# Nineteen folded columns a head for twenty: the last softmax feature of keys and queries set to one by GpSimd

## The chip, the cores and the metric

One core of a Trainium2 chip runs the whole program. The time is device microseconds of one execution, inputs and outputs in HBM; the figure of a kernel is the median over its runs. The core's engines, with the names that the profile uses: TensorE (PE, with its weight loads PEld), VectorE (DVE), ScalarE (ACT), GpSimd (POOL) and SyncE (SP, which here issues nearly all DMAs).

## The reference

Two residual blocks over x of 2048 tokens by 640: linear attention with a softmax feature map (32 heads of 20), then a dense SiLU block of width 1728.

```python
qkv = x @ wqkv                                  # layernormed x; 32 heads, Dh = 20
pq = jnp.einsum("bhsd,hdf->bhsf", q, w_phi)     # 20 features a head
pk = jnp.einsum("bhsd,hdf->bhsf", k, w_phi)
phi_q = concat([softmax(pq), softmax(-pq)])     # 40 features a head
phi_k = concat([softmax(pk), softmax(-pk)])
kv = jnp.einsum("bhsf,bhsd->bhfd", phi_k, v)
z  = jnp.einsum("bhsf->bhf", phi_k)
o  = (phi_q @ kv) / (phi_q . z + 1e-6)
h  = x + o.reshape(B, S, D) @ wo
out = h + silu(layernorm(h) @ w1) @ w2
```

## The kernel before, in words

The tokens are 16 tiles of 128. For each tile t the first part does: moments and normalization of x (`st`, `rs`, `xn`), a transpose into XnT (`xt`; by PE for the first four tiles, by a DMA on SP for the others), keys' features by PE (`K`), two exponentials of them by ACT (`ex`, exp and exp of the negative), the sums over each 20 by DVE (`su`), their inverse by ACT (`rk`), the scaling by DVE (`sc`), the values by PE with a copy by ACT (`V`, `ve`), and the product of scaled features and values, accumulated over all tiles in PSUM (`kv`). Queries go the same way (`Q`, `qe`, `qs`, `ql`, `qi`, `qr`, `qt`), then attention (`D`, `E`), the output projection (`ot`, `G`, `ga`), the second layernorm (`ls`, `lr`, `hn`, `ht`) and the dense block (`u`, `s`, `d`, `oa`, `out`).

The features need no separate step for w_phi: it is folded into the key and query columns of wqkv ahead of time. For keys, PE transposes Wk (`wk`), DVE builds a block-diagonal `phi` from w_phi (`phi_a`, `phi_b`), and PE multiplies both into Wfk (`fk`, copied by `fk..e`). For queries the same is done in six blocks of up to 120 columns: POOL builds `phi_q` (`phq`), PE multiplies with the DMA-transposed WTq (`fq`, L400), ACT or DVE copies into Wfq (`fq..e`, L406).

What is emitted when is written out by hand in ORDER, a list of step names; each step's instructions go to the in-order queues of their engines at that place, and semaphores for what one needs of another are set from the tiles that they read and write. So an instruction that waits holds whatever stands behind it on its engine. Of the steps around the change: xn3 to xn5 and xn7 to xn15 are on POOL, L450.

Buffers that matter here: the exponentials of a key tile go to `EK[t % 4]` (NE = 4), laid out as 64 runs of 20 features (32 heads, plus and minus) and a zeroed tail; `su` (L557) and `sc` (L570) work on all 20 of a run, and `kv` (L589) reads the scaled buffer as its weights. `VP[t % 8]` holds the values, with a column of ones for each head that POOL writes once for a buffer (`ones0` to `ones7`, L229); `kv` multiplies by it, so that z comes out beside kv. The queries' exponentials go to EQ, which has a place for each of the 16 tiles. PSUM has eight banks; until the queries' halves are used, `K`, `V`, `Q`, `fk` and `fq` take pairs of banks in turn out of three pairs, so that each waits for whoever reads the pair's content of three takers before.

Of the kernel before, what the change touches and what calls it, by code (L numbers as in the profile page):

```python
# [59 lines left out]
def kernel(  # L60
# [20 lines left out]
    DH = 20  # L81
    HF = 2 * DH
# [142 lines left out]
    Wfk = proj.tile([P, C, D], BF16, name="Wfk")  # L225
    Wfq = proj.tile([P, C, D + DH], BF16, name="Wfq")

    def ones(i):
        nc.gpsimd.memset(VP[i][:, :, DH:HV], 1.0)  # L229
        if i < NE:  # L230
            nc.gpsimd.memset(EK[i][:, H * HF :], 0.0)

# [25 lines left out]
    BW = 240  # L258

    PB = {0: (0, 240, 0), 1: (120, 260, BW), 2: (240, 400, 2 * BW), 3: (380, 520, 3 * BW + 20), 4: (400, 640, 4 * BW - 80)}  # L260
# [12 lines left out]
    nc.gpsimd.memset(phi[:, :, 8 * DH : BW], 0.0)  # L273
    ps_of = {}

    def phi_own(b):

        a, n = 3 * b, 3 - b
        engines[on(f"phi_{'ab'[b]}", "DVE")].tensor_tensor(
            phi[:, a : a + n, 0 : 8 * DH].rearrange("p r (h f) -> p r h f", f=DH),  # L280
            WPH[:, a : a + n].unsqueeze(2).to_broadcast([P, n, 8, DH]),
            own[:, a : a + n].unsqueeze(3).to_broadcast([P, n, 8, DH]), op=ALU.mult,
        )
# [53 lines left out]
    LW = D - (NQ - 1) * QW  # L337
    WPQ = early.tile([P, NQ, DH], BF16, name="WPQ")
    own_q = early.tile([P, 2, BH], BF16, name="own_q")
    phi_q = early.tile([P, NQ, QW], BF16, name="phi_q")  # L340
# [25 lines left out]
    def phi_blocks():  # L366

        n = NQ - 1
        nc.gpsimd.tensor_tensor(
            phi_q[0:QW, 0:n].rearrange("p r (h f) -> p r h f", f=DH),  # L370
            WPQ[0:QW, 0:n].unsqueeze(2).to_broadcast([QW, n, BH, DH]),
            own_q[0:QW, 0].unsqueeze(1).unsqueeze(3).to_broadcast([QW, n, BH, DH]), op=ALU.mult,
        )
        n = LW // DH
        nc.gpsimd.tensor_tensor(
            phi_q[P // 2 : P, NQ - 1, 0:LW].rearrange("p (h f) -> p h f", f=DH),
            WPQ[P // 2 : P, NQ - 1].unsqueeze(1).to_broadcast([P // 2, n, DH]),
            own_q[P // 2 : P, 1, 0:n].unsqueeze(2).to_broadcast([P // 2, n, DH]), op=ALU.mult,
        )
# [10 lines left out]
    def width(r):  # L390
        return min(QW, D - QW * r)
# [13 lines left out]
    def folded_block(eng, r):  # L405
        eng(Wfq[:, :, QW * r : QW * r + width(r)], ps_of.pop(("fq", r)))  # L406
# [12 lines left out]

    add("eqp", eq_pads)  # L420

# [71 lines left out]
    def project(t, W, key):  # L493

        ps = ps_of[key, t] = ps_pair()
        for g in range(2):
            for c in range(C):
                nc.tensor.matmul(  # L498
                    ps[:, g, 0:HD],
                    XnT[:, c, t * P : (t + 1) * P],  # L500
                    W[:, c, g * HD : (g + 1) * HD],
                    start=(c == 0),
                    stop=(c == C - 1),
                )
# [27 lines left out]
    def project_queries(t, g, ps):  # L532
        a, b = (DH * h for h in Q_PARTS[g])
        for c in range(C):
            e = b if c == 0 else min(b, D)
            nc.tensor.matmul(  # L536
                ps[:, 0 : e - a], XnT[:, c, t * P : (t + 1) * P], Wfq[:, c, a:e],
                start=(c == 0), stop=(c == C - 1),
            )
# [8 lines left out]
    def key_exps(t):  # L548
        ek[t] = EK[t % NE]
        p4 = ps_of.pop(("K", t))[:, :, 0:HD].rearrange("p g (h f) -> p g h f", f=DH)  # L550
        E5 = ek[t][:, 0 : H * HF].rearrange("p (g h b f) -> p g h b f", g=2, b=2, f=DH)
        for b, sign in ((0, 1.0), (1, -1.0)):
            nc.scalar.activation(E5[:, :, :, b, :], p4, AF.Exp, scale=sign)  # L553
# [51 lines left out]
    for t in range(T):  # L605
        if t == 0:
            add("K0s", first_key_bank)
            for c in range(C):
                add(f"K0.{c}", lambda c=c: first_key_chunk(c))
        else:  # L610
            add(f"K{t}", lambda t=t: project(t, Wfk, "K"))
        add(f"ex{t}", lambda t=t: key_exps(t))
        add(f"su{t}", lambda t=t: key_sums(t))
        add(f"rk{t}", lambda t=t: key_inverse(t))
        add(f"sc{t}", lambda t=t: key_scale(t))
        if t == 0:
# [27 lines left out]
    def query_exps(t):  # L644

        n = DH * HC
# [8 lines left out]
        for a, b, ps in parts:  # L655
            p4 = ps.rearrange("p (c h f) -> p c h f", h=HC, f=DH)
            for i, sign in ((0, 1.0), (1, -1.0)):
                nc.scalar.activation(features(t, a, b)[:, :, :, i], p4, AF.Exp, scale=sign)  # L658
# [308 lines left out]
```

## Time and profile before

| | |
|---|---|
| median of 3 runs | 235.19 us (235.07 to 235.41) |
| profiled execution, span from first to last instruction | 232.8 us |
| instructions | 5040 |
| HBM read, written | 9.64 MB, 2.62 MB |
| the first layer's key and value stage | about 12 to 67 us of the span |
| the queries' projections | about 42 to 87 us |
| the dense block | from about 91 us on |

In the profile's views a row of a group has line, engine, operation, out<-in with partitions x elements, the count, then busy time, the mean duration in ns of one, and the idle time before them with what ended it. A row of the chain of waits or of a timeline has start and length in us, what ran, and how many of them were merged. A row of the table by stretches gives, after the stretch and its length, the busy time and the instructions of PE, PEld, DVE, ACT and POOL, then the granted clock of PE, the DMA engines' share and GB/s. Durations of instructions that overlap in an engine's pipeline are longer than the steps from one to the next.

### The profile page before, as it was taken

The numbers are of one execution on the slowest core, as the hardware profiler recorded it, in microseconds if no ns is written. First come the engines' busy times: TensorE is split into PE (matmuls) and PEld (weight loads), VectorE is DVE, ScalarE is ACT, GpSimd is POOL, SyncE is SP. The second block draws the span as 40 slices with busy tenths as digits, with TensorE's granted clock in tenths as the row PEclk, the third lists the DMA queues.
The fourth block names the chain that finished last, engine by engine and source line by source line (L and its number), as shares of the span: only waits on it lengthen the run. The fifth ranks groups of instructions, "written<-read, shape, count | busy, mean of one in ns | idle before, by whom it ended". The sixth has DMA issues, their size and how long they took to land.

```text
span 232.8 us, 5040 instructions
## 1 busy us (share of the span) xinstructions
PE 228.0 (98%) x1977; PEld 160.5 (69%) x1984; DVE 164.0 (70%) x340; ACT 107.4 (46%) x241; POOL 62.6 (27%) x99
## 2 busy tenths in 40 slices
PE   7999999999999999999999999999999999999995
PEld 5777777777777778877545777655677455778874
DVE  4989999999999899998999794891472330404031
ACT  2899999998879884410344000064200235001400
POOL 7589896995001120211010111110020010100000
PEclk9999999999999999999999999999999999999999
DMA  6995379698836766696236956137213301011011
GB/s 169 336 291 103 87 119 217 217 145 188 220 115 114 159 116 136 124 121 146 56 66 154 120 114 158 30 80 172 55 28 85 99 0 28 31 28 56 8 56 56
DMA packets 67213, 26.79 MB, mean 115 GB/s; under 512 B 60151, under 2 KB 66167, under 8 KB 67063
## 3 DMA queue, kind: packets, MB, share of 16 engines
q1 hardware_dynamic: 66535, 26.47, 49.9%
q8 instruction: 15, 0.25, 0.5%
q10 hardware_dynamic: 656, 0.03, 0.2%
q14 instruction: 7, 0.06, 0.1%
HBM read 9.64 MB, written 2.62 MB: 53 GB/s over the span
## 4 chain that ended last, share of the span: by engine, by line
PE 95%; DMA 2%; SPq 1%; issue 1%; ACT 1%; DVE 0%
PE banks L890 24%; PE banks L850 24%; PE banks L498 18%; PE banks L536 9%; PE banks L767 9%; PE banks L589 2%; PE banks L734 2%; PE banks L893 2%; DMA Wk<-in_A_wqkv_dram 2%; PE banks L861 1%; PE banks L525 1%; PE banks L400 1%; ACT Wfk L325 1%; SPq L166 1%; PE banks L510 0%
## 5 line engine op out<-in xcount | busy, mean ns | idle before, releaser
L870 ACT ACTIVATE shT<-banks 128x512 bf16<-128x512 f32 (+1 forms) x53 | 28.5, 591 | 84.2 <-PE banks L850 84.2
L890 PE MATMUL banks<-w_sb,shT 128*128 128x320 bf16 (+2 forms) x429 | 61.3, 295 | 0.0
L850 PE MATMUL banks<-HnT,w_sb 128*128 128x512 bf16 (+1 forms) x318 | 58.4, 335 | 0.4
L890 PEld LDWEIGHTS <-shT 128*128 128x128 bf16 x429 | 41.1, 98 | 15.2
L850 PEld LDWEIGHTS <-w_sb 128*128 128x128 bf16 x325 | 31.2, 98 | 22.1
L899 DVE TENSOR_TENSOR o_t<-banks,X 128x320 bf16<-128x320 f32 (+2 forms) x33 | 14.9, 474 | 39.6 <-PE banks L893 26.7
L443 POOL TENSOR_SCALAR rs<-mv 128x1 f32<-128x1 f32 x21 | 5.8, 276 | 113.2 <-DVE mv L435 113.2
L498 PEld LDWEIGHTS <-XnT 128*128 128x128 bf16 x300 | 28.5, 98 | 10.3
L450 POOL TENSOR_SCALAR xn<-X,mv,rs 128x640 bf16<-128x640 bf16 x12 | 31.3, 2615 | 4.1 <-ACT rs L441 2.1
L434 DVE BATCH_NORM_STATS2 st<-X 128x6 f32<-128x320 bf16 x64 | 27.9, 477 | 4.3 <-DMA X<-in_A_x_dram 4.0
L767 PE MATMUL banks<-wo_sb,OT 128*128 128x320 bf16 x160 | 24.8, 299 | 0.0
L662 DVE TENSOR_REDUCE Sq<-EQ 128x66 f32<-128x1320 bf16 x16 | 23.9, 1512 | 0.0
L774 DVE TENSOR_TENSOR X<-banks,X 128x320 bf16<-128x320 f32 x32 | 14.7, 483 | 13.0 <-PE banks L767 12.9
L658 ACT ACTIVATE EQ<-banks 128x360 bf16<-128x360 f32 (+2 forms) x52 | 22.0, 514 | 3.2 <-PE banks L536 3.1
L557 DVE TENSOR_REDUCE Sk<-EK 128x64 f32<-128x1280 bf16 x16 | 23.3, 1468 | 0.2 <-ACT EK L553 0.2
L536 PE MATMUL banks<-Wfq,XnT 128*128 128x360 bf16 (+2 forms) x160 | 23.3, 299 | 0.0
L498 PE MATMUL banks<-Wv,XnT 128*128 128x320 bf16 x150 | 22.5, 299 | 0.0
L498 PE MATMUL banks<-Wfk,XnT 128*128 128x320 bf16 x150 | 22.5, 299 | 0.0
L553 ACT ACTIVATE EK<-banks 128x640 bf16<-128x640 f32 x32 | 20.5, 698 | 1.4 <-PE banks L498 1.2
L767 PEld LDWEIGHTS <-OT 128*128 128x128 bf16 x160 | 15.2, 98 | 6.5
L536 PEld LDWEIGHTS <-XnT 128*128 128x128 bf16 x160 | 15.2, 97 | 6.2
L747 DVE TENSOR_TENSOR O<-banks,Rd 128x360 bf16<-128x360 f32 (+1 forms) x32 | 15.7, 491 | 1.1
(76 smaller groups left out, 203.0 us busy)
## 6 DMA issues: line engine op xcount, KB each, us to landing
out_dram<-o_t SPq DMA_DIRECT2D x15, 160.0 KB, 2.0
w_sb<-in_B_w_dram SPq DMA_DIRECT2D x5, 432.0 KB, 4.8
w_sb<-in_B_w_dram SPq DMA_DIRECT2D x3, 480.0 KB, 4.1
X<-in_A_x_dram SPq DMA_DIRECT2D x1, 1280.0 KB, 8.4
Wk<-in_A_wqkv_dram SPq DMA_DIRECT2D x5, 160.0 KB, 3.8
Wv<-in_A_wqkv_dram SPq DMA_DIRECT2D x5, 160.0 KB, 4.9
wo_sb<-in_A_wo_dram SPq DMA_DIRECT2D x1, 800.0 KB, 6.5
X<-in_A_x_dram SPq DMA_DIRECT2D x1, 640.0 KB, 5.9
```

What stands on the lines that cost most here:

```text
L434: nc.vector.bn_stats(st[:, i, :], X[:, t, i * HD : (i + 1) * HD])
L450: eng.tensor_scalar(out=xn_[t][:], in0=X[:, t, :], scalar1=mv_.pop(t)[:, 0:1], scalar2=rs_.pop(t)[:], op0=ALU.subtract, op1=ALU.mult,)
L498: nc.tensor.matmul(ps[:, g, 0:HD], XnT[:, c, t * P : (t + 1) * P], W[:, c, g * HD : (g + 1) * HD], start=(c == 0), stop=(c == C - 1),)
L536: nc.tensor.matmul(ps[:, 0 : e - a], XnT[:, c, t * P : (t + 1) * P], Wfq[:, c, a:e], start=(c == 0), stop=(c == C - 1),)
L553: nc.scalar.activation(E5[:, :, :, b, :], p4, AF.Exp, scale=sign)
L557: nc.vector.tensor_reduce(sk[t][:], ek[t][:, 0 : H * HF].rearrange("p (q f) -> p q f", f=DH), axis=AX.X, op=ALU.add)
L658: nc.scalar.activation(features(t, a, b)[:, :, :, i], p4, AF.Exp, scale=sign)
L662: nc.vector.tensor_reduce(sq[t][:], EQ[0][:, t, :, 0:FCH].rearrange("p c (q f) -> p c q f", f=DH), axis=AX.X, op=ALU.add)
L767: nc.tensor.matmul(ps[:, 0:HD], ot[t][:, c, :], wo_sb[:, c, g * HD : (g + 1) * HD], start=(c == 0), stop=(c == C - 1),)
L850: nc.tensor.matmul(ps[:, at : at + n], w1_sb[:, c, fc * P : fc * P + P], HnT[u][:, c, 0:n], start=(c == 0), stop=(c == C - 1),)
L870: nc.scalar.activation(shT[u][:, f0 * n : f1 * n], ps_of.pop(("u", u, f0))[:, 0 : (f1 - f0) * n], AF.Silu)
L890: nc.tensor.matmul(ps[:, 0 : b - a], shT[u][:, at : at + P], w2_sb[:, fc, a:b], start=(fc == 0), stop=False,)
```

## The change

A softmax does not change when the same number is taken from all its inputs. The change takes the head's last feature from the other nineteen, in the folded weights: `w_phi[:, f] - w_phi[:, 19]` for f under 19. The twentieth feature's exponent is then 0 and its exponential 1, for both signs. So the folded weights have 19 columns a head, 608 for 640, `K` multiplies 304 columns a half for 320 and `Q` 342 and 285 or 266 for 360 and 300 or 280; the exponentials write 19 of each run of 20; and POOL writes the ones.

New on POOL: `reference_feature` memsets 64 columns (one of each 20, stride 20) of a key buffer. It runs in `ones0` to `ones3` for the first use of each buffer, and, since `sc` scales the ones too, again for each of tiles 4 to 15, as the new steps `ref4` to `ref15`, which ORDER has right behind `kv0` to `kv11`. `eqr` memsets the 1056 columns of EQ once for all query tiles, behind `fq5e`. `phq` has two subtractions more on POOL (95 and 19 elements), and `phi_a` one on DVE (95 elements). Nothing is removed but columns; the sums, scales, products with values and everything behind them keep their sizes.

```diff
-load10 kv0 ones2 xn6 K4 ex4 V4 sc1 fq3 ones7 ve4 rs8 kv1 xn7 xt5 wq0 xn8 xn9 fq3e xt6 V5 su2 xt7 wq5 rk2
-su3 ve5 rk3 wq4 K5 sc2 ex5 fq0 K6 kv2 sc3 st11 kv3 fq0e xt8 fq2 ex6 st10 su4 fq2e su5 rs11 V6 ve6 st13
+load10 kv0 ref4 ones2 xn6 K4 ex4 V4 sc1 fq3 ones7 ve4 rs8 kv1 ref5 xn7 xt5 wq0 xn8 xn9 fq3e xt6 V5 su2 xt7 wq5 rk2
+su3 ve5 rk3 wq4 K5 sc2 ex5 fq0 K6 kv2 ref6 sc3 st11 kv3 ref7 fq0e xt8 fq2 ex6 st10 su4 fq2e su5 rs11 V6 ve6 st13
 fq1 K7 st14 V7 fq1e rk4 xt9 rs10 xn10 ex7 zeros ve7 su6 rs13 V8 sc4 ve8 fq4 V9 ones4 load0 xt10 load5
-fq5 fq4e rk5 rk6 su7 ve9 K8 sc5 xn11 kv4 load7 fq5e rs14 K9 rk7 sc6 rs12 ex8 kv5 Q0 sc7 ex9 qe0 xn14
-ones6 K10 su8 xt11 xn12 kv6 load2 xn13 su9 st15 rs15 kv7 qs0 xt12 xn15 Q1 rk8 V10 ex10 sc8 qe1 ve10
-load3 ql0 K11 V11 xt13 rk9 ex11 qs1 su10 qi0 ve11 ql1 eqp rk10 kv8 K12 V12 ex12 qi1 sc9 ve12 load4 su11
-sc10 kv9 K13 rk11 V13 kv10 qr0 xt14 K14 su12 ex13 rk12 sc11 su13 ve13 xt15 ex14 rk13 K15 kv11 V14 Q2
+fq5 fq4e rk5 rk6 su7 ve9 K8 sc5 xn11 kv4 ref8 load7 fq5e eqr rs14 K9 rk7 sc6 rs12 ex8 kv5 ref9 Q0 sc7 ex9 qe0 xn14
+ones6 K10 su8 xt11 xn12 kv6 ref10 load2 xn13 su9 st15 rs15 kv7 ref11 qs0 xt12 xn15 Q1 rk8 V10 ex10 sc8 qe1 ve10
+load3 ql0 K11 V11 xt13 rk9 ex11 qs1 su10 qi0 ve11 ql1 eqp rk10 kv8 ref12 K12 V12 ex12 qi1 sc9 ve12 load4 su11
+sc10 kv9 ref13 K13 rk11 V13 kv10 ref14 qr0 xt14 K14 su12 ex13 rk12 sc11 su13 ve13 xt15 ex14 rk13 K15 kv11 ref15 V14 Q2
...
+    DR = DH - 1
+    HR = H // 2 * DR
+    DP = H * DR
...
-    Wfk = proj.tile([P, C, D], BF16, name="Wfk")
-    Wfq = proj.tile([P, C, D + DH], BF16, name="Wfq")
+    Wfk = proj.tile([P, C, DP], BF16, name="Wfk")
+    Wfq = proj.tile([P, C, DP + DR], BF16, name="Wfq")
+
+    def reference_feature(i):
+
+        r = EK[i][:, 0 : H * HF].rearrange("p (q f) -> p q f", f=DH)
+        nc.gpsimd.memset(r[:, :, DR:DH], 1.0)
...
         if i < NE:
             nc.gpsimd.memset(EK[i][:, H * HF :], 0.0)
+            reference_feature(i)
...
+    WPD = early.tile([P, C, DR], BF16, name="WPD")
...
+        if b == 0:
+            nc.vector.tensor_tensor(
+                WPD[:], WPH[:, :, 0:DR], WPH[:, :, DR:DH].to_broadcast([P, C, DR]), op=ALU.subtract
+            )
...
+        for rows, r in ((slice(0, QW), slice(0, n)), (slice(P // 2, P), slice(n, NQ))):
+            w = WPQ[rows, r]
+            nc.gpsimd.tensor_tensor(
+                WPQD[rows, r], w[:, :, 0:DR], w[:, :, DR:DH].to_broadcast([rows.stop - rows.start, r.stop - r.start, DR]),
+                op=ALU.subtract,
+            )
...
+    def eq_references():
+        r = EQ[0][:, :, :, 0:FCH].rearrange("p t c (q f) -> p (t c) q f", f=DH)
+        nc.gpsimd.memset(r[:, :, :, DR:DH], 1.0)
...
+    add("eqr", eq_references)
...
-            nc.scalar.activation(E5[:, :, :, b, :], p4, AF.Exp, scale=sign)
+            nc.scalar.activation(E5[:, :, :, b, 0:DR], p4, AF.Exp, scale=sign)
...
+        if t >= NE:
+            add(f"ref{t}", lambda t=t: reference_feature(t % NE))
...
-                nc.scalar.activation(features(t, a, b)[:, :, :, i], p4, AF.Exp, scale=sign)
+                nc.scalar.activation(features(t, a, b)[:, :, :, i, 0:DR], p4, AF.Exp, scale=sign)
```

More of the change, by code (lines that the diff above doesn't have):

```diff
@@ L272 @@
     )
-    nc.gpsimd.memset(phi[:, :, 8 * DH : BW], 0.0)
+    nc.gpsimd.memset(phi[:, :, 8 * DR : BW], 0.0)
+    WPD = early.tile([P, C, DR], BF16, name="WPD")
     ps_of = {}
@@ L337 @@
     LW = D - (NQ - 1) * QW
+    QR = BH * DR
     WPQ = early.tile([P, NQ, DH], BF16, name="WPQ")
     own_q = early.tile([P, 2, BH], BF16, name="own_q")
-    phi_q = early.tile([P, NQ, QW], BF16, name="phi_q")
+    WPQD = early.tile([P, NQ, DR], BF16, name="WPQD")
+    phi_q = early.tile([P, NQ, QR], BF16, name="phi_q")
     WTq = early.tile([P, NQ, D], BF16, name="WTq")
@@ L375, in phi_blocks @@
         nc.gpsimd.tensor_tensor(
[L376 to L378 removed]
+            phi_q[P // 2 : P, NQ - 1, 0 : n * DR].rearrange("p (h f) -> p h f", f=DR),
+            WPQD[P // 2 : P, NQ - 1].unsqueeze(1).to_broadcast([P // 2, n, DR]),
+            own_q[P // 2 : P, 1, 0:n].unsqueeze(2).to_broadcast([P // 2, n, DR]), op=ALU.mult,
         )
@@ L644, in query_exps @@
     def query_exps(t):
-        n = DH * HC
+        n = DR * HC
         if ("Q", t) in ps_of:
```

53 lines of the change are left out of this document (28 added, 25 removed).

## The prediction

> **What bounds the kernel now.** I read the page's busy times and chain first, then a table by stretches, then the chain in order of time and the timelines of GpSimd (POOL) and ScalarE (ACT) between 20 and 60 us.
>
> ```profile
> PE 228.0 (98%) x1977; PEld 160.5 (69%) x1984; DVE 164.0 (70%) x340; ACT 107.4 (46%) x241; POOL 62.6 (27%) x99
> PE 95%; DMA 2%; SPq 1%; issue 1%; ACT 1%; DVE 0%
> 12.00:70.00 58.00, 58.00 (x600) 43.86 (x598) 55.40 (x81) 53.18 (x124) 40.16 (x31) 1.00 0.72 168
> ```
>
> The last row gives the stretch from 12 to 70 us: TensorE (PE) busy for all 58.00, VectorE (DVE) 55.40, ACT 53.18, POOL 40.16, clock 1.00. So PE sets the end, and every column taken from its matmuls is worth its time; but in the key and value stage three engines are nearly full beside it, and whatever holds one of them soon reaches PE.
>
> **What the narrower columns give.** From the chain (start, length, line, count):
>
> ```profile
> 3.11 4.05 DMA Wk<-in_A_wqkv_dram
> ...
> 16.66 5.43 PE banks L498 x40
> ...
> 41.87 1.37 PE banks L536 x10
> ...
> 211.55 5.46 PE banks L850 x50
> ```
>
> A matmul of 320 columns takes 5.43/40 = 136 ns; the 50 of L850 here are the last unit's, of 256 columns, at 109 ns. That is 0.42 ns a column. Keys: 160 matmuls lose 16 columns each, 6.7 ns, 1.07 us in all. Queries: each tile's ten lose 160 together, 67 ns of the row's 1.37 us, 1.07 us over 16 tiles. The two foldings lose some 230 and 160 columns, 0.16 us. Sum: 2.3 us.
>
> ```profile
> L553 ACT ACTIVATE EK<-banks 128x640 bf16<-128x640 f32 x32 | 20.5, 698 | 1.4 <-PE banks L498 1.2
> L279 DVE TENSOR_TENSOR phi<-WPH,own 128x480 bf16<-128x480 bf16 (+1 forms) x2 | 1.0, 551 | 0.0
> ```
>
> ACT's exponentials shrink by 5% too (608 elements for 640, some 30 of 698 ns), which PE does not wait for. DVE's sums and scales keep 20 columns. DVE's new subtraction near 4 us (95 elements) costs 0.1 to 0.25 us, by elements or half of L279's mean; two key memsets in ones0 and ones3 stand before the first rs on POOL, another 0.2 or so. The chain there is the landing of Wk, until 7.16 us, which covers both; uncovered they would cost up to 0.5.
>
> **What the memsets cost themselves.** No row shows a memset of 64 single columns, or of 1056. The nearest:
>
> ```profile
> L229 POOL MEMSET VP<- 128x32 bf16 x8 | 1.8, 253 | 0.1
> L418 POOL MEMSET EQ<- 128x1408 bf16 x1 | 1.3, 1270 | 0.0
> L369 POOL TENSOR_TENSOR phi_q<-WPQ,own_q 120x600 bf16<-120x600 bf16 x1 | 1.3, 1328 | 0.0
> ```
>
> VP's 32 elements are single columns too: I take 0.25 us for a key tile's 64, between that row (0.25) and 64/600 of the phi_q row plus its (0.4). EQ's 1056 single columns: 0.95 us by L418's 0.9 ns an element, 2.3 us by phi_q's 2.2 ns; I take 0.95, since L229 shows that single columns are no dearer. The two subtractions of phi_blocks: 0.7 us from phi_q's row and its overheads, bounds 0.3 and 1.3. Twelve memsets, 3 us, would hide in POOL's 18 idle us. Their place is the matter.
>
> **Where they stand.** POOL runs in order. A key buffer's memset may run only after kv of the tile four earlier has read it on PE, and in the built program the first exponential of the next tile in it (and its sum on DVE) waits for the memset. So POOL waits for PE at each, with the normalizations (xn) behind it, and ACT waits for POOL.
>
> ```profile
> 22.42 0.26 POOL L375 TENSOR_TENSOR phi_q<-WPQ,own_q 64x40 bf16<-64x40 bf16 x1
> ...
> 22.86 0.30 POOL L229 MEMSET VP<- 128x32 bf16 x1
> 23.92 8.04 POOL L450 TENSOR_SCALAR xn<-X,mv,rs 128x640 bf16<-128x640 bf16 x3 [0.76 <-DVE xn L450]
> ...
> 32.92 2.52 POOL L450 TENSOR_SCALAR xn<-X,mv,rs 128x640 bf16<-128x640 bf16 x1
> ...
> 35.53 2.50 POOL L450 TENSOR_SCALAR xn<-X,mv,rs 128x640 bf16<-128x640 bf16 x1
> 40.11 3.14 POOL L450 TENSOR_SCALAR xn<-X,mv,rs 128x640 bf16<-128x640 bf16 x1 [2.08 <-ACT rs L441]
> 43.20 0.24 POOL L229 MEMSET VP<- 128x32 bf16 x1
> 43.30 4.98 POOL L450 TENSOR_SCALAR xn<-X,mv,rs 128x640 bf16<-128x640 bf16 x2
> 48.26 0.89 POOL L443 TENSOR_SCALAR rs<-mv 128x1 f32<-128x1 f32 x1
> ...
> 49.90 2.51 POOL L450 TENSOR_SCALAR xn<-X,mv,rs 128x640 bf16<-128x640 bf16 x1
> 52.38 0.41 POOL L682 TENSOR_TENSOR Rho<-Sq,Rq 128x66 bf16<-128x66 f32 x1
> 52.73 1.27 POOL L418 MEMSET EQ<- 128x1408 bf16 x1
> ```
>
> ```profile
> 25.41 0.34 PE banks L589 x11
> ...
> 32.39 0.26 PE banks L400 x5
> 32.66 4.08 PE banks L498 x30
> ...
> 39.84 0.33 PE banks L589 x11
> ...
> 41.53 0.34 PE banks L589 x11
> ...
> 44.60 0.67 PE banks L589 x22
> ...
> 46.64 4.07 PE banks L498 x30
> ...
> 54.11 2.72 PE banks L498 x20
> ```
>
> ```profile
> 30.46 1.30 ACT L553 ACTIVATE EK<-banks 128x640 bf16<-128x640 f32 x2
> 31.65 0.67 ACT L406 CAST Wfq<-banks 128x600 bf16<-128x600 f32 x1
> ...
> 45.19 1.28 ACT L553 ACTIVATE EK<-banks 128x640 bf16<-128x640 f32 x2
> ...
> 52.45 1.30 ACT L553 ACTIVATE EK<-banks 128x640 bf16<-128x640 f32 x2
> ```
>
> An aside on L589: it reads 63 columns from multiples of 63, odd starts among them, at 0.33/11 = 30 ns; so the odd starts of blocks of 19 get no price.
>
> The walk, in times of before plus shifts (refN is the memset before tile N, exN its exponentials):
>
> First pause. ref5 waits for kv1 (PE 25.41 to 25.75, now some 0.4 earlier, plus about 0.15 until its results are told): POOL, free at 23.2 (23.9 with the two subtractions, which this wait covers), goes on at 25.6. xn7 to xn9 take their 8.04 to 33.65 in place of 31.96. Only then comes ref6, done at 33.9, although kv2 was long over. ex6, at 30.46 before, starts at 33.93 and ends, 1.24 later, at 35.17. The block fq1 (PE, 32.39) takes the banks that ex6 reads: it starts at 35.2, **2.8 us late**. PE, which would have been there at 31.8, stands for 3.4. ACT's next cast (fq2e, 31.65) ends at 35.7, and K7 (32.66) needs its banks: 35.75, 3.1 late.
>
> Second pause. kv4 (39.84) ends near 43.1, with 0.13 gained from K7 and K8. ref8 waits for it from 39.8 on, the memset of EQ follows (to 44.4), and ref9 waits for kv5 (41.53, now 44.4 to 44.8). xn14 starts at 45.07, 4.96 late, and ones6 (43.20) behind it at 48.2; kv6 (44.60) multiplies by those ones: 48.43, **3.8 late**, a pause of 1.1.
>
> Third and fourth. ref10 stands behind xn12 (half of the 4.98): 50.7; ex10 (45.19) at 51.0 ends at 52.2, and K11 (the second ten of the row at 46.64, so 48.00) takes its banks at 52.26: 4.3 late, a pause of 0.5. POOL stays 5 us behind: xn13, rs15, ref11, xn15, the ratio, the pads (52.73 + 5 + 1.24) and then ref12 at 58.94; ex12 (52.45) from 59.2 to 60.5; V13 (second ten of the row at 54.11, so 55.47) takes its banks at 60.5: **5.0 late**, a pause of 1.0.
>
> After that the last two key tiles and 14 query tiles give 16 x 67 ns = 1.07 back, and PE never has to wait for these memsets again. XnT's transposes on SP follow xn, 1.7 and then 5 us late, where PE itself is 2.8 and then 4 to 5 late, so I put no further wait there. Sum of the pauses: 3.4 + 0.3 + 1.1 + 0.5 + 1.0 = 6.3; less 2.3 of columns: **+4.0 us**. The profiled execution's span of 232.8 becomes 236.8; the median of the runs, 235.19, lies 2.4 above that span, and so 239.2 is the forecast.
>
> **The rivals.**
>
> (1) *Faster, PE alone decides.* If the memsets land ahead of their exponentials everywhere, the time is 235.2 - 2.3 = 232.9. For it: PE is busy for the whole stretch and all POOL's additions together are about 5 us. It is decided at ref6: it must be done by about 30.5, but the row at 23.92 ends at 31.96 even undelayed. The no-change case needs the first pause halved and the other three gone.
>
> (2) *Shorter pauses.* Two xn take 4.98 in the row at 43.30, 2.49 each, where three take 8.04. If the delayed ones meet less of DVE's work and take 2.5 all, 0.55 falls from the first pause and 0.65 from the second: +2.8, 238.0.
>
> (3) *Dear single columns.* At phi_q's 2.2 ns an element EQ's memset takes 1.4 more and each key memset 0.1 to 0.15; the first and third pauses take 0.1 each, the second 1.4, the fourth 0.2: +5.8, 241.0. L229 speaks against it.
>
> (4) *A slow restart.* After the pause of 3.4 us PE's matmuls may run slower for a while.
>
> ```profile
> 0.82 3.36 PE L217 MATMUL banks<-const-bfloat16-1.0 128*128 128x256 bf16 x15 [0.82 <-PEq L951]
> ...
> 4.42 0.72 PE L217 MATMUL banks<-const-bfloat16-1.0 128*128 128x256 bf16 x5
> ```
>
> ```profile
> PE banks L292 <- DMA Wk<-in_A_wqkv_dram: 0.6, 2, 0.4
> ```
>
> The first 15 take some 210 ns each where 256 columns take 109 ns later: 1.7 us lost after the idle start. The same loss after the first pause makes 240.9. No row shows how long an idle stretch brings it on (PE's longest wait here after the start, in the list of waits, is this row's 0.4 us). The Trainium skill, in "TensorE: Matmul & The Clock Gate", Part 1 (The HAM clock gate), says that the clock halves once a free-running window of about 3.4 us passes idle; the pause has about that length, so by that rule it needs the window to fall exactly on it, and the trace neither confirms nor denies the threshold.
>
> **How the numbers follow.** The walk as it stands, from 238.5 to 240.0: 0.60. Rival 2: 0.17. Rivals 3 and 4: 0.08 each. Rival 1: 0.05, with 0.02 for no change. A difference under 0.2% (0.5 us) can't be told from none here. Slower: 0.60 + 0.17 + 0.08 + 0.08 = 0.93; same 0.02; faster 0.05. The range, 237.2 to 241.2, takes in rivals 2, 3 and 4, and leaves out rival 1 and a slow restart on top of dear memsets.
>
> **What would show it.** In the profile after: matmuls of 304 columns at 129 ns; POOL idle before a memset of EK, released by L589's line, near 23.8 and 40; the memset of ref6 behind three xn near 33.7; ACT idle for 3 to 4 us before an exponential, released by POOL; PE idle near 32 to 35 us before a block of the query folding, and again near 47 us before kv6 with VP's memset as the releaser. The forecast is wrong if ex6 starts near 30.5, if PE shows no pause over 1 us after 12 us, or if matmuls keep 136 ns.

## The result, and the profile after

The changed kernel takes 244.9 us (median of 4 runs, 243.94 to 245.32) where the kernel before, on the same chip, takes 235.3 (235.07 to 236.1): 1.040 times as long, with an interval of 1.037 to 1.043. The profiled execution has a span of 243.0 us, 10.2 over before's, and a mean granted clock of 0.979 in place of 1.00. The forecast of 239.2 had the direction; 244.9 lies 3.7 above the range's upper end.

From the page of the changed kernel, the busy times and the first row of its chain:

```profile
PE 231.3 (95%) x1984; PEld 162.1 (67%) x1984; DVE 164.7 (68%) x341; ACT 105.8 (44%) x241; POOL 69.6 (29%) x118
...
PE 81%; POOL 5%; DVE 5%; DMA 3%; issue 3%; ACT 2%; SPq 0%; POOLq 0%; DVEq 0%; ACTq 0%
```

PE falls from 98% of the span to 95% and in the chain from 95% to 81%, and its busy time grows by 3.3 us although its matmuls became narrower. So there are pauses and there are slower matmuls. The list of waits of the changed kernel (us in total, times, longest) names the pauses:

```profile
ACT EK L583 <- POOL EK L234: 11.5, 6, 4.4
...
PE banks L425 <- ACT EK L583: 3.6, 1, 3.6
PE banks L619 <- POOL VP L237: 3.6, 1, 3.6
...
PEld L619 <- DVE EK L600: 0.4, 1, 0.4
```

L425 is a block of the query folding (L400 before), L619 is `kv`, L583 the keys' exponentials, L234 the new memset of EK, L237 the ones of VP. The timelines of POOL and ACT around both places:

```profile
25.58 0.38 POOL L234 MEMSET EK<- 128x64 bf16 x1 [1.53 <-PE banks L619]
26.06 8.02 POOL L480 TENSOR_SCALAR xn<-X,mv,rs 128x640 bf16<-128x640 bf16 x3
34.03 0.65 POOL L234 MEMSET EK<- 128x64 bf16 x2
...
37.92 0.12 POOL L260 MEMSET Wfq<- 128x19 bf16 x1
...
46.48 0.38 POOL L234 MEMSET EK<- 128x64 bf16 x1 [5.92 <-DMA w_sb<-in_B_w_dram]
46.66 4.90 POOL L447 MEMSET EQ<- 128x1056 bf16 x1
51.14 0.70 POOL L234 MEMSET EK<- 128x64 bf16 x1
51.47 2.50 POOL L480 TENSOR_SCALAR xn<-X,mv,rs 128x640 bf16<-128x640 bf16 x1
53.91 0.25 POOL L237 MEMSET VP<- 128x32 bf16 x1
```

```profile
34.44 1.29 ACT L583 ACTIVATE EK<-banks 128x608 bf16<-128x608 f32 x2 [4.36 <-POOL EK L234]
```

The first pause is the walk's: ref5 waits for kv1 until 25.58, three xn take 8.02, ref6 stands behind them at 34.03, ex6 behind it at 34.44 (forecast 33.93). The second has the walk's chain as well (ref8, EQ's memset, ref9, xn14, ones6, kv6), but EQ's memset takes 4.90 us where 0.95 was put in. Ahead of ref8 the row at 46.48 names a DMA; kv4, the row at 45.92 below, ended at 46.42, and in the run with the memsets alone the same memset is released by kv's line (44.00, idle 3.51), so I read kv4 here too. What TensorE makes of it:

```profile
35.77 0.64 PE L425 MATMUL banks<-phi_q,WTq 128*128 128x114 bf16 x5 [3.58 <-ACT EK L583]
36.29 2.69 PE L528 MATMUL banks<-Wfk,XnT 128*128 128x304 bf16 x10
38.77 4.28 PE L528 MATMUL banks<-Wv,XnT 128*128 128x320 bf16 x20
42.89 0.41 PE L425 MATMUL banks<-phi_q,WTq 128*128 128x114 bf16 x5
...
45.92 0.50 PE L619 MATMUL banks<-VP,EK 128*128 128x63 bf16 x11
...
54.21 0.83 PE L619 MATMUL banks<-VP,EK 128*128 128x63 bf16 x22 [3.56 <-POOL VP L237]
54.89 2.37 PE L566 MATMUL banks<-Wfq,XnT 128*128 128x342 bf16 x10
...
61.87 0.50 PE L619 MATMUL banks<-VP,EK 128*128 128x63 bf16 x11
...
68.19 2.74 PE L528 MATMUL banks<-Wfk,XnT 128*128 128x304 bf16 x20
70.77 0.50 PE L619 MATMUL banks<-VP,EK 128*128 128x63 bf16 x11
```

At 68.19, 20 matmuls of 304 columns take 2.58 us to the next row: 129 ns each, as forecast. At 36.29, behind the first pause, ten take some 2.5: twice as long. The table by stretches (columns as in the prediction's) has the reason in its third column from the right:

```profile
32.00:36.00 4.00, 0.42 (x5) 0.23 (x3) 3.93 (x9) 1.56 (x3) 3.79 (x6) 0.85 0.62 129
36.00:40.00 4.00, 4.00 (x20) 2.42 (x18) 2.71 (x3) 3.13 (x9) 4.00 (x4) 0.50 0.79 230
40.00:44.00 4.00, 4.00 (x29) 2.64 (x27) 1.49 (x1) 2.35 (x6) 0.56 (x1) 0.80 0.96 283
...
52.00:56.00 4.00, 1.79 (x28) 1.34 (x28) 2.71 (x5) 2.78 (x6) 4.00 (x3) 0.91 0.00 0
56.00:60.00 4.00, 4.00 (x23) 2.57 (x22) 2.75 (x3) 3.06 (x5) 3.92 (x6) 0.66 0.41 107
```

The granted clock is halved for 2 x (0.15 + 0.50 + 0.20) x 4 = 6.8 us around the first pause and for 2 x (0.09 + 0.34) x 4 = 3.4 us behind the second.

Where the 10.2 us come from, by comparing starts in the timelines of TensorE before and after: block fq1 starts at 35.77 for 32.23, 3.54 late; the block fq4, behind V8, at 42.89 for 36.57, 6.32 late, so the half clock cost 2.78, and 2.85 with K7's own 0.07 of columns. kv6 starts at 54.21 for 44.43, 9.78 late; kv8 at 61.87 for 50.55, 11.32 late: 1.54, or 1.67 with the columns of Q1 and K11. Pauses 3.58 and 3.56, a wait of 0.4 at kv1, half clock 2.85 and 1.67: 12.1. The remainder to 10.2, 1.9 us, I put down to the columns; a run below measures them apart.

### The profile page after: what moved, and what is told of

Same layout as the page of the kernel before. It is cut to its first block, busy times and chain, and to the rows that moved or that the text cites. A ratio compares the mean times of both kernels' runs of the same rounds, so it can differ in the third digit from the quotient of the medians.

```text
span 243.0 us, 5092 instructions
## 1 busy us (share of the span) xinstructions
PE 231.3 (95%) x1984; PEld 162.1 (67%) x1984; DVE 164.7 (68%) x341; ACT 105.8 (44%) x241; POOL 69.6 (29%) x118
## 4 chain that ended last, share of the span: by engine, by line
PE 81%; POOL 5%; DVE 5%; DMA 3%; issue 3%; ACT 2%; SPq 0%; POOLq 0%; DVEq 0%; ACTq 0%
PE banks L922 23%; PE banks L882 23%; PE banks L528 9%; PE banks L799 9%; PE banks L566 8%; POOL xn L480 4%; PE banks L766 2%; DMA w_sb<-in_B_w_dram 2%; PE banks L925 2%; PE banks L619 1%; DVE Sk L587 1%; DVE st L464 1%; DMA X<-in_A_x_dram 1%; PE banks L893 1%; ACT Wfk L342 1%
## 5 line engine op out<-in xcount | busy, mean ns | idle before, releaser
L528 PEld LDWEIGHTS <-XnT 128*128 128x128 bf16 x300 | 29.9, 102 | 11.8 <-DMA XnT<-xn 0.2
L473 POOL TENSOR_SCALAR rs<-mv 128x1 f32<-128x1 f32 x21 | 5.0, 239 | 111.9 <-DVE mv L465 111.9
L480 POOL TENSOR_SCALAR xn<-X,mv,rs 128x640 bf16<-128x640 bf16 x12 | 30.8, 2566 | 0.9 <-ACT rs L471 0.6
L583 ACT ACTIVATE EK<-banks 128x608 bf16<-128x608 f32 x32 | 20.3, 692 | 12.7 <-POOL EK L234 11.5
L528 PE MATMUL banks<-Wv,XnT 128*128 128x320 bf16 x150 | 24.7, 318 | 0.0
L566 PE MATMUL banks<-Wfq,XnT 128*128 128x342 bf16 (+2 forms) x160 | 23.2, 300 | 0.0
L528 PE MATMUL banks<-Wfk,XnT 128*128 128x304 bf16 x150 | 22.7, 303 | 0.0
L690 ACT ACTIVATE EQ<-banks 128x342 bf16<-128x342 f32 (+2 forms) x52 | 21.5, 514 | 1.6 <-PE banks L566 1.6
L566 PEld LDWEIGHTS <-XnT 128*128 128x128 bf16 x160 | 15.4, 99 | 5.8
```

Of the source, the lines that this page charges most:

```text
L480: eng.tensor_scalar(out=xn_[t][:], in0=X[:, t, :], scalar1=mv_.pop(t)[:, 0:1], scalar2=rs_.pop(t)[:], op0=ALU.subtract, op1=ALU.mult,)
L528: nc.tensor.matmul(ps[:, g, 0:w], XnT[:, c, t * P : (t + 1) * P], W[:, c, g * w : (g + 1) * w], start=(c == 0), stop=(c == C - 1),)
L566: nc.tensor.matmul(ps[:, 0 : e - a], XnT[:, c, t * P : (t + 1) * P], Wfq[:, c, a:e], start=(c == 0), stop=(c == C - 1),)
L583: nc.scalar.activation(E5[:, :, :, b, 0:DR], p4, AF.Exp, scale=sign)
L690: nc.scalar.activation(features(t, a, b)[:, :, :, i, 0:DR], p4, AF.Exp, scale=sign)
```

## The experiments

There are two questions: whether the pauses come from the memsets alone, and what each of the three unforeseen terms (clock, price of EQ's memset, wait at kv1) is worth. All times are device microseconds; "before" is 234.6 to 235.1 in all of these comparisons.

**The memsets without the columns.** The kernel before with its 20 columns, and the memsets of ones at the change's places. They come ahead of the exponentials, which write all 20 again; only in tile 2 the memset comes behind, so that its twentieth feature is 1.

```diff
...
-load10 kv0 ones2 xn6 K4 ex4 V4 sc1 fq3 ones7 ve4 rs8 kv1 xn7 xt5 wq0 xn8 xn9 fq3e xt6 V5 su2 xt7 wq5 rk2
+load10 kv0 ref4 ones2 xn6 K4 ex4 V4 sc1 fq3 ones7 ve4 rs8 kv1 ref5 xn7 xt5 wq0 xn8 xn9 fq3e xt6 V5 su2 xt7 wq5 rk2
...
+        nc.gpsimd.memset(r[:, :, DH - 1 : DH], 1.0)
...
+        nc.gpsimd.memset(r[:, :, :, DH - 1 : DH], 1.0)
...
```

> The kernel before with the memsets alone: ref4 to ref15, the four first ones and EQ's 1056 columns stand where the change has them, but features keep 20 columns (the exponentials overwrite the ones) and there are no subtractions. Theory (queue): POOL's memsets, held by kv and holding xn, make both pauses of TensorE and the two stretches at half clock by themselves, so the loss is the change's plus the 2.2 us that its narrower columns give back: 246 to 248 us, pauses near 3.6 us at the query folding before K7 and at kv6. Rival (columns): if odd starts or runs of 19 cost something of their own, the memsets alone lose less than the change: under 244.5 us.

Measured: 245.81 us (243.48 to 246.81), 1.045 of before [1.039, 1.051]; profiled span 241.5, clock 0.993. Its timeline of TensorE:

```profile
35.72 0.42 PE L406 MATMUL banks<-phi_q,WTq 128*128 128x120 bf16 x5 [3.46 <-ACT EK L564]
...
37.62 2.88 PE L509 MATMUL banks<-Wv,XnT 128*128 128x320 bf16 x20
...
51.73 1.30 PE L600 MATMUL banks<-VP,EK 128*128 128x63 bf16 x22 [3.36 <-POOL VP L234]
```

Both pauses are there, so the memsets and their places bring them, not the narrower columns or the subtractions. The time is just under the expected 246 to 248, and at 1.3 us over the rival's bound; the executions differ too much in their clock for it to price the columns. In the profiled one the clock fell behind the second pause only: the 20 matmuls of V take 2.88 us at 37.62, against 4.28 in the changed kernel. The four executions separate the clock's price: those with a mean clock of 0.993, 0.986, 0.979 and 0.979 took 243.48, 245.02, 246.60 and 246.81. A step of 0.007 of some 242 us is 1.7 us of lost clock, that is one stretch of 3.4 us at half, and each more of them costs 1.5 to 1.8 us in this kernel.

**EQ's memset cut in two.** The changed kernel; 132 columns (tiles 0 and 1) at the old place, 924 behind mask1, where POOL has nothing to do.

```diff
...
-    def eq_references():
-        r = EQ[0][:, :, :, 0:FCH].rearrange("p t c (q f) -> p (t c) q f", f=DH)
+    def eq_references(a, b):
+        r = EQ[0][:, a:b, :, 0:FCH].rearrange("p t c (q f) -> p (t c) q f", f=DH)
...
-    add("eqr", eq_references)
+    add("eqr", lambda: eq_references(0, 2))
+    add("eqr2", lambda: eq_references(2, T))
```

> The change with EQ's memset cut in two: tiles 0 and 1 (132 columns) at its place, the other 924 behind mask1, where POOL has time. Theory (4.5 ns a column holds xn14 and ones6): the second pause falls from 3.6 to about 1 us and its half clock goes: 4 us less, 240 to 242 us, the first pause as it was. Rival (the second pause comes from ref8 and ref9 waiting for kv4 and kv5): pause over 3 us, 244 us and more.

Measured: 240.13 us (239.6 to 241.05), ratio 1.023 [1.019, 1.026]. POOL, then TensorE:

```profile
44.80 0.79 POOL L447 MEMSET EQ<- 128x132 bf16 x1
```

```profile
34.84 0.41 PE L425 MATMUL banks<-phi_q,WTq 128*128 128x114 bf16 x5 [2.94 <-ACT EK L584]
...
49.11 0.83 PE L620 MATMUL banks<-VP,EK 128*128 128x63 bf16 x22 [0.32 <-POOL VP L237]
...
53.11 1.45 PE L529 MATMUL banks<-Wfk,XnT 128*128 128x304 bf16 x10 [0.50 <-ACT EK L584]
...
61.00 1.52 PE L529 MATMUL banks<-Wv,XnT 128*128 128x320 bf16 x10 [0.46 <-ACT EK L584]
```

The time and the second pause are as the theory had them. With a memset of 0.79 us at that place, near the 0.95 of the forecast, the second pause is 0.32 (forecast 1.1), and the third and fourth, at K11 and at V13, appear with 0.50 and 0.46 (forecast 0.5 and 1.0). K7 starts 0.51 us after fq1 where 0.26 is usual, 0.25 for the forecast's 0.3. So the walk had the places right for the memset that it assumed, and its sizes came out smaller: 4.5 us of pauses in all for 6.3. That the time is only 0.9 above the forecast is partly chance, since each execution (clock 0.992 to 0.993) has one stretch of half clock in it, which the forecast had not.

**Two columns a place.** What makes single columns dear was tried in the five-buffer kernel described below: EQ's later memset sets the eighteenth and the nineteenth feature at each of its 924 places; the queries' exponentials write the eighteenth again.

```diff
-        nc.gpsimd.memset(r[:, :, :, DR:DH], 1.0)
+        nc.gpsimd.memset(r[:, :, :, (DR if a == 0 else DR - 1) : DH], 1.0)
```

> The five-buffer run with EQ's second memset (tiles 2 to 15, 924 single columns, 4.22 us) setting two adjoining columns in place of one at each of the 924 places; the eighteenth feature's column is written again by the queries' exponentials. One reading (the price is per place, by the stride): the memset stays within 4.0 to 4.8 us. The other (the price is per element at 4.5 ns, whatever adjoins): 8.2 to 8.6 us. The time is not the question here: 233 to 236 us.

Both readings missed. The row without and the row with the edit:

```profile
58.12 4.22 POOL L447 MEMSET EQ<- 128x924 bf16 x1
```

```profile
57.67 1.77 POOL L447 MEMSET EQ<- 128x1848 bf16 x1
```

Twice the elements take 0.42 of the time: 4.57 ns for a column that stands alone, 0.96 ns an element in pairs (1.92 a place). The time, 233.52 in one run, is as without the edit (233.46). These pairs begin at an even column and EQ's single ones stand at an odd one, which no run tried apart. One row speaks against the odd column as the reason: the memsets of 64 and of 924 single columns, 0.38 and 4.22 us, give some 4.5 ns a column and 0.1 us fixed, and by that VP's 32, which stand 21 apart and so at even and odd columns in turn, would take 0.24 by this estimate; they took 0.24 to 0.25.

**Pairs in the changed kernel, nothing moved.** EQ's memset and those of ref4 to ref15 set two columns, all ahead of the exponentials that write the first of the two.

```diff
-    def reference_feature(i):
+    def reference_feature(i, n=2):
...
-        nc.gpsimd.memset(r[:, :, DR:DH], 1.0)
+        nc.gpsimd.memset(r[:, :, DH - n : DH], 1.0)
...
-            reference_feature(i)
+            reference_feature(i, 1)
...
-        nc.gpsimd.memset(r[:, :, :, DR:DH], 1.0)
+        nc.gpsimd.memset(r[:, :, :, DR - 1 : DH], 1.0)
```

> The changed kernel, every step in its place, with EQ's memset and the keys' memsets from tile 4 on setting two adjoining columns (the eighteenth feature and the nineteenth) at each of their places; the exponentials write the eighteenth again afterwards. Theory (the second pause is the price of single columns: 4.22 us for 924 of them against 1.77 us for 924 pairs): EQ's memset 1.9 to 2.2 us in place of 4.90, the pause at kv6 falls from 3.56 us to 0.2 to 0.7 us, the first pause stays at 3.0 to 3.5 us since three xn still stand ahead of its memset, the clock falls once; 239.5 to 241 us. Rival (the place counts, not the price: kv6 waits whatever the memset takes): the second pause stays over 2 us and the time over 242.5 us.

Measured: 239.74 us (239.38 to 240.33), ratio 1.020 [1.017, 1.023]; POOL and TensorE:

```profile
44.51 2.00 POOL L447 MEMSET EQ<- 128x2112 bf16 x1
```

```profile
34.55 0.41 PE L425 MATMUL banks<-phi_q,WTq 128*128 128x114 bf16 x5 [2.72 <-ACT EK L583]
...
49.37 0.83 PE L619 MATMUL banks<-VP,EK 128*128 128x63 bf16 x22 [0.86 <-POOL VP L237]
```

2.00 us at the very place where 4.90 stood bring a pause of 0.86 for 3.56, a little over the 0.2 to 0.7 expected: the price made the second pause. (The keys' memsets, now 0.21 us for 0.38, can have only a small part in it.) The first stays, with 2.72 somewhat under the expected 3.0 to 3.5, since three xn still stand ahead of ref6.

**The clock: matmuls that only fill the pauses.** Two runs put matmuls ahead of fq1 and of kv6, into columns of PSUM that nothing reads. The first had 36 on a constant:

```diff
-fq1 K7 st14 V7 fq1e rk4 xt9 rs10 xn10 ex7 zeros ve7 su6 rs13 V8 sc4 ve8 fq4 V9 ones4 load0 xt10 load5
+fill0 fq1 K7 st14 V7 fq1e rk4 xt9 rs10 xn10 ex7 zeros ve7 su6 rs13 V8 sc4 ve8 fq4 V9 ones4 load0 xt10 load5
...
-ones6 K10 su8 xt11 xn12 kv6 ref10 load2 xn13 su9 st15 rs15 kv7 ref11 qs0 xt12 xn15 Q1 rk8 V10 ex10 sc8 qe1 ve10
+ones6 K10 su8 xt11 xn12 fill1 kv6 ref10 load2 xn13 su9 st15 rs15 kv7 ref11 qs0 xt12 xn15 Q1 rk8 V10 ex10 sc8 qe1 ve10
...
+        for _ in range(36):
+            nc.tensor.matmul(
+                kv_ps[:, 0, 384:512], warm_t[:, 0:P], warm_t[:, 0:P], start=False, stop=False, skip_group_check=True,
+            )
...
```

> The change with 36 matmuls of 128 columns without use ahead of the block fq1 and 36 ahead of kv6, into columns of the kv banks that nothing reads: at 55 ns each they take 2.0 us of each pause and leave about 1.6 us idle. They do not move what ends the pauses. Theory (idle time halves the clock): the granted clock stays 1.00 and the 2.5 and 1.5 us lost at half clock come back: 240 to 241.5 us. Rival (the clock falls for another reason, or the lost time was hidden by POOL's lateness): clock under 0.99 again, or 243.5 us and more.

Measured: 242.65 us (241.62 to 244.15), ratio 1.033 [1.028, 1.039]. The two executions with a clock of 1.000 took 241.62 and 241.80, those with 0.992 took 243.50 and 244.15: the first pair lies just above the theory's range, the second has the rival's time. Two rows of the profiled one, which is of the second kind:

```profile
36.18 0.41 PE L434 MATMUL banks<-phi_q,WTq 128*128 128x114 bf16 x5 [1.66 <-ACT EK L592]
```

```profile
36.00:40.00 4.00, 3.72 (x19) 2.30 (x19) 3.06 (x4) 3.34 (x10) 4.00 (x4) 0.62 0.77 226
```

So a rest of 1.66 us, behind 2.28 us of matmuls on a constant, was still followed by the half clock in this execution. Whether the length of the rest or the constant data counted is not separated, for the second run changed both. It had 60 on real data:

```diff
...
+        for _ in range(60):
+            nc.tensor.matmul(
+                kv_ps[:, 0, 384:512], XnT[:, 0, 0:P], Wv[:, 0, 0:P], start=False, stop=False, skip_group_check=True,
+            )
...
```

> The changed kernel with 60 matmuls of 128 columns of real data (XnT by Wv, about 3.2 us, into columns of PSUM that nothing reads) ahead of block fq1 and again ahead of kv6, in place of most of the two pauses. Theory (the time over the pauses themselves is the granted clock, which falls after a pause): idle time of TensorE under 0.6 us at each place, clock 1.00 throughout, span 238.5 to 239.5, time 240.5 to 241.5 us and a spread between runs under 0.6 us. Rival (what is lost besides the pauses is something other than the clock): 243.5 us or more with the clock at 1.00.

Measured: 242.54 us (241.78 to 243.92), ratio 1.031 [1.027, 1.036], clock 0.999 to 1.000 in all four, between the two expectations. TensorE:

```profile
31.78 3.51 PE L229 MATMUL banks<-Wv,XnT 128*128 128x128 bf16 x60
35.60 0.41 PE L434 MATMUL banks<-phi_q,WTq 128*128 128x114 bf16 x5 [0.30 <-ACT EK L592]
...
51.45 0.83 PE L628 MATMUL banks<-VP,EK 128*128 128x63 bf16 x22 [0.23 <-POOL VP L246]
...
55.45 1.45 PE L537 MATMUL banks<-Wfk,XnT 128*128 128x304 bf16 x10 [0.50 <-ACT EK L592]
...
63.35 1.52 PE L537 MATMUL banks<-Wv,XnT 128*128 128x320 bf16 x10 [0.47 <-ACT EK L592]
```

With the clock kept, the median falls by 2.4 us from the changed kernel's 244.9, less than the 4.5 that the half clock cost in the profiled execution. Three of the changed kernel's four executions had a clock of 0.986, one stretch fewer than the profiled one; and here the third and fourth pauses are back (0.50 and 0.47), which do not show in the changed kernel. The spread of 2.1 us, expected under 0.6, does not come from the clock, and need not come from the change: the kernel before spread by as much in the same comparison (234.46 to 236.48, clock 0.999 to 1.000). Its cause stays open.

**A fifth key buffer.** With NE = 5 the memset for tile N waits for kv of tile N - 5, and the walk's first condition is gone: ref6 no longer needs to stand behind three xn. The remaining memsets were placed anew, EQ's cut as above.

```diff
-load10 kv0 ref4 ones2 xn6 K4 ex4 V4 sc1 fq3 ones7 ve4 rs8 kv1 ref5 xn7 xt5 wq0 xn8 xn9 fq3e xt6 V5 su2 xt7 wq5 rk2
+load10 kv0 ref5 ones2 ones4 xn6 K4 ex4 V4 sc1 fq3 ones7 ve4 rs8 kv1 xn7 ref6 xt5 wq0 xn8 xn9 fq3e xt6 V5 su2 xt7 wq5 rk2
...
-    NE = 4
+    NE = 5
...
```

> The change with five key buffers, so that each memset may run a tile earlier, ref5 to ref15 put in POOL's order where kv is over and xn is not held, ones4 moved ahead, and EQ's memset in two as in the split run. Theory (placement is all): no pause of TensorE over 0.5 us after 12 us, clock 1.00, and the columns' 2.2 us show: 232.8 to 233.8 us, ratio 0.99. Rival (memsets on POOL or odd columns cost by themselves): 235 us and more.

Measured: 234.36 us (233.85 to 235.72), ratio 0.999 [0.997, 1.001], clock 1.00, between the two expectations. Both long pauses are gone, but only part of the columns' gain is left. VectorE and the list of waits:

```profile
22.92 1.79 DVE L481 TENSOR_SCALAR xn<-X,mv,rs 128x640 bf16<-128x640 bf16 x1
```

```profile
PE banks L620 <- DVE EK L601: 0.7, 1, 0.7
```

The same xn6 before the change and in the changed kernel:

```profile
23.43 0.45 DVE L450 TENSOR_SCALAR xn<-X,mv,rs 128x640 bf16<-128x640 bf16 x1
```

```profile
22.89 1.33 DVE L480 TENSOR_SCALAR xn<-X,mv,rs 128x640 bf16<-128x640 bf16 x1
```

In the changed kernel and here it ends 0.18 us after the last of a train of memsets on POOL (five there, eight here), and here kv1 waits 0.7 us for the multiply behind it. That is the 0.4 of the changed kernel, with more memsets in the train. A wait of 0.5 us for a transfer of XnT comes on top here.

**The memsets away from xn6.** Four of these steps moved (ones2 ahead of ex0, ones4 and ref5 behind xn7, ones7 behind ref8), and EQ's first part, with ref9 behind it, stands behind fq5e.

```diff
...
-load10 kv0 ref5 ones2 ones4 xn6 K4 ex4 V4 sc1 fq3 ones7 ve4 rs8 kv1 xn7 ref6 xt5 wq0 xn8 xn9 fq3e xt6 V5 su2 xt7 wq5 rk2
+load10 kv0 xn6 K4 ex4 V4 sc1 fq3 ve4 rs8 kv1 xn7 ones4 ref5 ref6 xt5 wq0 xn8 xn9 fq3e xt6 V5 su2 xt7 wq5 rk2
...
-fq5 fq4e rk5 rk6 su7 ve9 K8 sc5 xn11 kv4 ref9 load7 fq5e rs14 K9 rk7 sc6 rs12 ex8 kv5 Q0 sc7 ex9 qe0 xn14
+fq5 fq4e rk5 rk6 su7 ve9 K8 sc5 xn11 kv4 load7 fq5e eqr ref9 rs14 K9 rk7 sc6 rs12 ex8 kv5 Q0 sc7 ex9 qe0 xn14
...
```

> The changed kernel with five buffers for the keys' exponentials and features in place of four, so that four memsets of ones stand where VectorE's xn6 is not running; EQ's memset cut in two, the part for tiles 0 and 1 into GpSimd's idle time before kv4 ends, the part for tiles 2 to 15 behind mask1. Theory (the columns are worth 2.3 us, all else that the change cost was GpSimd's order): xn6 back from 1.79 us to about 0.45, no idle time of TensorE at kv1 over 0.1 us, granted clock 1.00 throughout, time 232.5 to 233.3 us against 235, ratio about 0.990. Rival (the queues' order takes back what TensorE saves, at the transposes of xn too): the ratio stays at 0.997 to 1.000, with TensorE waiting 0.4 us or more for an XnT transfer near 54 us and for VectorE near 25 us.

Measured: 233.46 us (233.19 to 234.23), ratio 0.993 [0.990, 0.995], span 231.9:

```profile
23.45 0.45 DVE L481 TENSOR_SCALAR xn<-X,mv,rs 128x640 bf16<-128x640 bf16 x1 [0.51 <-ACT rs L472]
```

xn6 is back at 0.45 and kv1 waits no more, as the theory had it; now kv4 waits 0.7 us for its multiply, and the time lies just above the expected 232.5 to 233.3.

**The same with 20 columns.** The kernel before with that run's order, buffers and memsets (seven buffers for V in place of eight, so without ones7; in tile 4 the memset comes behind the exponentials, so that its twentieth feature is 1).

> The kernel before (20 columns a head, no subtraction) with the memsets of ones, the five buffers and the order of the run beside it; the copies of V have seven buffers in place of eight, for space. What differs from that run is the columns and the three subtractions alone. Theory: TensorE needs the time of before, so 234.8 to 235.6 us (ratio 0.998 to 1.002), and the run with 19 columns is 2.0 to 2.4 us below it. Rival (the columns are hidden behind other work): less than 0.8 us between the two.

Measured: 234.93 us (234.35 to 237.56), ratio 1.001 [0.998, 1.004]; profiled span 233.8. The spans differ by 1.9 us, the medians by 1.5; each of the two profiles has one wait of 0.7 to 0.8 for a multiply of VectorE, at different places, and near the start the one with 19 columns also waits 0.8 us for Wv, the one with 20 waits 0.5 for Wk. So the columns are worth 1.5 to 1.9 us, good to some tenths: less than the 2.0 expected at least, and far from the rival's 0.8.

**What is left.** Two runs tried to win kv4's wait back. With the pairs in the five-buffer kernel:

> The five-buffer run with its four memsets out of VectorE's way, with pairs of columns in EQ's two memsets and in the keys' from tile 5 on. Theory (VectorE's multiply before kv4 took 1.35 us in place of 0.81 because memsets of single columns ran beside it, and kv4 waited 0.7 us for it): the keys' memset near 0.2 us in place of 0.38, the multiply back to 0.8 to 0.9, kv4's wait under 0.3 us, 232.7 to 233.2 us. Rival (the multiply is slowed by the xn that GpSimd runs beside it): the wait stays at 0.6 to 0.8 us and the time at 233.3 to 233.6 us.

Measured: 233.28 us (233.06 to 234.87), ratio 0.993 [0.990, 0.996], span 231.4. The multiply still takes longer:

```profile
39.92 1.27 DVE L601 TENSOR_TENSOR EK<-EK,Rk 128x1280 bf16<-128x1280 bf16 x1
```

The keys' memset fell to 0.21 us as the theory had it, but it was not what slowed the multiply, and kv4's wait stays at 0.65: the rival's account. POOL's xn began at 39.65, just ahead of it; but a multiply that began 1.3 us after another xn, at 37.80, took 0.82 while that xn still ran, so the xn as such doesn't explain it either, and this stays open. Then the multiply was moved ahead of the sum su6:

```diff
-fq1 K7 st14 V7 fq1e rk4 xt9 rs10 xn10 ex7 zeros ve7 su6 rs13 V8 sc4 ve8 fq4 V9 load0 xt10 load5
-fq5 fq4e rk5 rk6 su7 ve9 K8 sc5 xn11 kv4 load7 fq5e eqr ref9 rs14 K9 rk7 sc6 rs12 ex8 kv5 Q0 sc7 ex9 qe0 xn14
+fq1 K7 st14 V7 fq1e rk4 xt9 rs10 xn10 ex7 zeros ve7 sc4 su6 rs13 V8 ve8 fq4 V9 load0 xt10 load5
+fq5 fq4e rk5 ve9 rk6 su7 K8 sc5 xn11 kv4 load7 fq5e eqr ref9 rs14 K9 rk7 sc6 rs12 ex8 kv5 Q0 sc7 ex9 qe0 xn14
```

> The run with five buffers and pairs of columns, with VectorE's multiply that kv4 waits for moved ahead of a sum (su6), whose factors ScalarE has ready 1.4 us before, and ScalarE's copy of V9 moved ahead of the inverse that waits for that sum. Theory (kv4 waits for its multiply alone, which stands behind su6 and then runs beside GpSimd's xn): no idle time of TensorE over 0.2 us at kv4, and 232.3 to 232.9 us, ratio 0.988 to 0.991. Rival (su6, now 0.8 us later, is late for kv5 or for the exponential of tile 8 instead): an idle time of 0.3 us or more within the next 5 us, and 233.0 us or more.

Measured: 233.53 us (232.82 to 234.68), ratio 0.995 [0.993, 0.997], span 231.9. kv4 waits no longer, but twelve microseconds later, beyond where either theory looked, stands

```profile
54.01 1.46 PE L529 MATMUL banks<-Wfk,XnT 128*128 128x304 bf16 x10 [1.17 <-ACT Rk L597]
```

whose weight load waits 1.3 us for an XnT transfer by the list of waits ("PEld L529 <- DMA XnT<-xn: 1.3"). The transfers of XnT between 48 and 56 us took up to 6.0 us from issue to landing here, 3.9 at most in the run without the move; whether the move brought that is not shown. So what one wait gave back another took; the three five-buffer versions from 233.28 to 233.53 can't be told apart.

## Why the prediction was wrong, step by step

- *The mechanism was right.* POOL runs in order, held by kv at each memset; ref6 stood behind three xn (34.03, forecast 33.65), ACT waited 4.36 us for it, and the first pause was 3.58 us (forecast 3.4). kv6 waited for ones6, with VP's memset as the releaser. The run with the memsets alone shows both without the narrower columns.
- *The step that failed first: "I take 0.95, since L229 shows that single columns are no dearer".* It took 4.90 us. L229's 0.253 us for 32 columns looked cheap because so few columns stand in it beside a fixed part. A row of the timeline of before shows that part, with 0.12 us for 20 adjoining elements:

```profile
35.38 0.12 POOL L251 MEMSET Wfq<- 128x20 bf16 x1
```

The rest, (0.253 - 0.12)/32, is 4.2 ns a column, and 1056 of them are 4.4 us. The price was in the profile of before, in the very row that was held against rival 3, and L418's 0.9 ns belongs to runs of adjoining elements. Even the upper bound, 2.3, from an operation of another kind, was too low. It made the second pause 3.56 in place of 1.1; 2.00 us at the same place made it 0.86. The pause grew by less than the price because the memset also covered ref9's wait for kv5, and because xn14 took 2.50 us for the 3.14 taken from before: this half of rival 2 came, the other did not (three xn took 8.02).
- *The second: the slow restart with 0.08 as a rival by itself.* It should have been a term of the sum at each long pause. The half clock cost 2.85 and 1.67 us where it stood, in the profiled execution; kept away by filling, the net is 2.4 between medians. The forecast put it at nothing; the rival priced it at 1.7 for one pause (1.5 by its own 210 and 109 ns) and at none for the other, and the range left out rivals 3 and 4 together, which is what came.
- *The third and fourth pauses* did not come in the changed kernel. They are missing in the two profiles with a stretch of half clock behind the second pause (the changed kernel and the memsets alone) and there in the four without it: 0.50 and 0.46 with EQ's memset cut, 0.32 and 0.30 with pairs, some 0.5 each with the constant fill, 0.50 and 0.47 with real data. So that stretch hides them, presumably because a slower PE lets POOL catch up. The third had its forecast size, the fourth half. K7's extra came as 0.25 where the clock was whole; behind the changed kernel's first pause it can't be told from the half clock.
- *"Covered": VectorE's xn6.* The walk looked at POOL's memsets for POOL's queue alone. Beside a train of them VectorE's xn6 took 1.33 us in place of 0.45, and kv1 stood 0.4 us. This wait comes and goes: in other runs that keep the changed kernel's order up to here, xn6 took 0.91 us (constant fill) and 0.40 (real data, and pairs in place), so the 0.4 need not stand in every execution.
- *The columns* have the forecast rate (129 ns a matmul) and gave 1.5 to 1.9 by the pair of runs (1.9 as the remainder of the sum above), for 2.3. A key memset took 0.38 us, inside the bounds of 0.25 to 0.4, and the two subtractions 0.64 for 0.7.

The sum put right, in us of the profiled execution: forecast +4.0; second pause +2.5; half clock +4.5; first pause +0.2 and kv1 +0.4; third, fourth and K7's -1.8; columns +0.4: +10.2. The columns' term being the remainder, this sum closes by construction. The median moved by 9.6 where the span moved by 10.2: the profiled execution took 2.05 us more than its span, and the forecast had added 2.4.

## What to carry to other kernels

Before a small operation's row is used as a price by element, take off what an operation of its kind costs with next to nothing in it: a row of 0.25 us can hide 4 ns an element. Pauses of TensorE of 2.7 to 3.6 us mostly cost more here than their length, so a walk that finds one should add the slow stretch behind it as a term, at 1.5 to 1.8 us each, or at least as part of the range. And a cheap column is only a gain where the engine that fills it in has somewhere to stand: here the change pays (0.993) with one more key buffer, EQ's ones set late, and the memsets kept clear of VectorE's xn6.

## What the runs showed of the hardware

- A memset of bf16 columns that stand alone, 20 apart, took GpSimd 4.6 ns a column; two adjoining columns took 1.9 ns together (4.22 us for 924 elements, 1.77 for 1848). Setting more was the cheaper way; why is not shown.
- The granted clock fell to half during or after pauses of 2.7 to 3.6 us, and in one profile after a rest of 1.66 us behind a fill, for stretches of 3.4 us each, one or two in a row. The kernel with the memsets alone had one, two or three such stretches in different executions by its mean clock, and a pause of 3.46 us passed without one. With the pauses filled with real data the clock stayed at 0.999 to 1.000. The Trainium skill, "TensorE: Matmul & The Clock Gate", Part 1 (The HAM clock gate), has a free-running window of about 3.4 us and a fall after an idle one. The length of the stretches and the chance in it agree; that the window must be wholly idle does not, since pauses of 2.72 and 2.94 us, which can't fill one, and the rest of 1.66 had their fall too.
- VectorE's xn6 (a tensor_scalar) went from 0.45 us to 1.33 and 1.79 while GpSimd ran a train of memsets, and ended 0.18 us after the last of them; in the run with real data, begun at the same distance ahead of the train (0.17 us), it took 0.40 and the first memset 0.56 for 0.38. The Trainium skill, "SBUF — State Buffer", section "Who interferes with whom", has the two engines share a pair of ports that whoever issues first holds for its whole instruction, and names tensor_scalar among those that can take it. These rows agree that one of the two waits, and that it can be either; that xn6 waited through a whole train of memsets is more than one instruction's hold and stays unexplained.
